# Two linear-attention and gated layers on one core: x-first loads, Strassen products for K in layer two, and earlier heads of the gate/up stages

## The chip, the cores and the metric

The kernel runs on one core of a Trainium2 chip. The number is device time in microseconds (us), from the first to the last instruction of one execution with what lies around it; lower is better. The core has a matrix engine (TensorE, PE in the profile; its weight loads are PEld), VectorE (DVE), ScalarE (ACT), GpSimd (POOL) and SyncE (SP), whose queue issues all DMAs of this kernel. Each engine works through its own list of instructions in order and waits on semaphores.

## What is computed

```python
def _A_ref(x, wqkv, wo):          # S = 2048, D = 1024, 32 heads of 32
    q, k, v = split(x @ wqkv)
    phi = lambda t: jnp.where(t > 0, t + 1, jnp.exp(t)) + 1e-6
    pq, pk = phi(q), phi(k)
    kv = einsum("bhsd,bhse->bhde", pk, v)
    z = einsum("bhsd->bhd", pk)
    o = einsum("bhqd,bhde->bhqe", pq, kv) / (einsum("bhqd,bhd->bhq", pq, z)[..., None] + 1e-6)
    return o @ wo
def _B_ref(x, w_gate, w_up, w_down):   # F = 3584
    return ((x @ w_gate) * (x @ w_up)) @ w_down
x = x + _A_ref(_layernorm(x), A_wqkv, A_wo)
x = x + _B_ref(_layernorm(x), B_w_gate, B_w_up, B_w_down)
x = x + _A_ref(_layernorm(x), A_wqkv, A_wo)
x = x + _B_ref(_layernorm(x), B_w_gate, B_w_up, B_w_down)
```

## The kernel before

The 2048 tokens are 16 tiles of 128. The normalised x is kept transposed in SBUF (`xnT`), x itself in `x_res`, all of it inside one array, `arena`; PSUM (`ps`) has eight banks of 512 columns. The kernel is one long Python program: `P.add(engine, ...)` appends an instruction to an engine's list, with the bytes and banks that it reads and writes, and a planner places the waits. So the order of the calls is the order on each engine, and nothing else decides it. The weights' rows and columns are cut into 2 x 2 blocks, and most large products are made by Winograd's form of Strassen's method: seven block products (1, 5, 6, 2, 7, 3, 4 in the order used) in place of eight, with sums of blocks prepared on DVE.

**Layer A, first time** (`layer_A`, `first`). Tile by tile, K and Q are made with plain products of eight matmuls for each half of 512 columns (`proj`, L949 to L957), phi is taken out of PSUM by `phi_evac` (L649): an exponential of each half on ACT, a minimum on DVE, and one DVE instruction for each half that takes the maximum with 0 and adds. `z_add` (L971) adds K's phi to a running sum on POOL. Layernorm runs ahead, in steps: `start` (two `bn_stats` halves, their aggregate, two short POOL instructions), `b_one` (the normalisation), `step_t` (the transposes on PE and a copy on ACT, later a DMA transpose). `lnstep` (L1220) places these steps around the K products. At the very start SP issues x tile 0 in halves, then k0, x1, k1, x2, q0, x3, q1 and the rest of x (L2182 to L2196); k0, k1, q0, q1 are the column halves of the K and Q weights, 1 MB each, and a tile of x is 256 KB. `pt_ops` (L1246) makes the four sums of Q's weights on DVE during the K products of tiles 4 to 7 and stores them (2 MB, `pt_scratch`) for layer two; the buffer is the one that V's weights are loaded into later (`load_w("v")`, L1280).

**Layer A, second time** (`kq_pairs`, L997 to L1201). Tiles go in pairs. K pairs are plain (`plain`, L1053): four steps of eight matmuls; both halves of a tile are evacuated together, as 128x1024 (`fin2`, L1033). Seven of the Q pairs are Strassen pairs (`strassen`, L1100): seven steps of four matmuls on banks A, B, C, Dk. Step 1's result is copied by ACT from A to B, step 5's to SBUF (`p5`), steps 6 and 7 add into B and DVE joins B and `p5` into Dk and C (`join`, L1118), and each half is evacuated alone (`fin1`, L1045) because `SEP` names Q. `s_sums` (L1080) makes the sums of x blocks for two pairs, four DVE instructions, into the places of `x_res` that are free. The exponentials go through four buffers (`ebuf`, L1019). Every step gets a position, the steps are sorted by it and called (L1172 to L1200); `flow_step` places layernorm's steps and `xr_load` the loads of normalised x for the next stage in the same list. `KSTR` chooses Strassen for K; it is off. What this stage reads is loaded during the end of the layer before (`dticks1`, L2121), behind the down product "3".

**Then** come the products of G (`gchunk`, 16 matmuls each), their use with V's weights (`kvt`), and y, attention's output: for each tile two groups of eight matmuls (`y_grp`, L1379) in the loop at L1399. During that loop layernorm for the gate/up stage runs, and `x_budget` makes the sums of x blocks on DVE from a list (`XQ`).

**Layer B** (`layer_B`): `gateup` runs a hand-written order of tokens (`ORDERS`): P, D and M are products and evacuations of first-level blocks, "11", "16", "17" and the like steps of a product that is itself a Strassen product (second level, 256 columns, L1540), S their sums, T the ticks of other work, R loads of the next weights. A "+" means the next pair. The tokens before the first pair's main work are a head (`pro`), which `pro_step` issues one PE instruction group at a time inside the stage before: one call in the last step of the y loop, three in the last products of the first `down` of layer two. In layer one's first half the head is empty (`jit`). `down` multiplies by w_down, partly with two levels (`two_level`, L1886).

## Time and profile before

| what | value |
|---|---|
| median of 3 runs | 1447.18 us (1445.64 to 1447.4) |
| the profiled execution | 1446.97 us, span 1445.2 us |
| TensorE's granted clock | 1.000 |
| PE busy, DVE busy | 1433.9 us, 1128.6 us |
| ACT busy, POOL busy | 680.2 us, 227.5 us |
| first K product of layer one | 7.93 us |
| K/Q stage of layer two | 737 to 835 us |

The profile is of one execution. A timeline row gives the start in us from the span's start, the duration in us, the engine, the line of the program, the operation, output and input with their shape, and in brackets the idle time before it and what ended it; "x8" merges eight such instructions. A row of the chain of waits has start, duration, engine and line. A row of a group has the busy time in us and the mean of one in ns. A row of a table of stretches has the stretch, its length, the busy time of PE, PEld, DVE, ACT and POOL with their instructions, the granted clock, the mean busy share of the DMA engines and GB/s. A matmul's duration contains its way through the array; the next one starts earlier than it ends, so a hole in PE is read from start to start.

### The profile page before, as it was taken

Reading aid. Unit: us, or ns where it says so; the run is one execution under the profiler, and the core shown is the slowest. Engines: PE = TensorE matmul, PEld = TensorE weight load, DVE = VectorE, ACT = ScalarE, POOL = GpSimd, SP = SyncE. Lnnn points to the kernel's source line nnn. Section 1 sums busy time; section 2 is a strip of 40 time slices with the busy share of each in tenths; the row PEclk is TensorE's granted clock in tenths of the full one; section 3 lists DMA queues with packets and bytes.
Section 4 is the critical chain, followed back from the end, with each engine's and each line's share of the span. In section 5 each row is a group of like instructions: output and inputs, shape, how many; then the busy total and the mean of one; then the engine's idle time right before and its main releaser. Section 6 shows DMA issues by size and latency. Waiting matters only on the chain.

```text
span 1445.2 us, 21993 instructions
## 1 busy us (share of the span) xinstructions
PE 1433.9 (99%) x8294; PEld 800.4 (55%) x8294; DVE 1128.6 (78%) x2027; ACT 680.2 (47%) x1438; POOL 227.5 (16%) x260
## 2 busy tenths in 40 slices
PE   8999999999999999999999999999999999999999
PEld 3444444555544555554664444456666457666547
DVE  6766889889867799877677779879877786777856
ACT  3652256677720255550156423567777005777401
POOL 4543733000000000000044346300000000000000
PEclk9999999999999999999999999999999999999999
DMA  6334757987879899986896067679975779887657
GB/s 233 88 79 118 151 125 155 290 298 249 294 288 338 262 271 294 293 257 225 253 341 195 0 173 151 155 213 274 282 260 197 241 247 296 264 264 257 205 164 239
DMA packets 377993, 324.41 MB, mean 224 GB/s; under 512 B 178208, under 2 KB 326048, under 8 KB 377632
## 3 DMA queue, kind: packets, MB, share of 16 engines
q1 hardware_dynamic: 377888, 323.02, 74.5%
q8 instruction: 65, 1.06, 0.3%
q14 instruction: 40, 0.33, 0.1%
HBM read 237.24 MB, written 62.13 MB: 207 GB/s over the span
## 4 chain that ended last, share of the span: by engine, by line
PE 92%; DVE 4%; DMA 2%; ACT 1%; issue 0%; SPq 0%; POOL 0%; DVEq 0%
PE ps L1470 25%; PE ps L1540 17%; PE ps L2020 16%; PE ps L1291 8%; PE ps L954 6%; PE ps L1383 6%; PE ps L1918 6%; PE ps L945 4%; PE ps L1115 3%; DVE arena L821 2%; DVE arena L824 1%; DMA arena<-in_A_wqkv_dram 1%; DMA arena<-in_B_w_up_dram 1%; DMA arena<-in_B_w_down_dram 1%; PE ps L1303 0%
## 5 line engine op out<-in xcount | busy, mean ns | idle before, releaser
L821 DVE TENSOR_TENSOR arena<-arena 128x512 f16<-128x512 f16 (+7 forms) x752 | 414.1, 577 | 75.9 <-ACT arena L1584 47.6
L1470 PE MATMUL ps<-arena 128*128 128x512 f16 x1808 | 446.5, 379 | 0.7 <-ACT ps L1500 0.7
L824 DVE SCALAR_TENSOR_TENSOR arena<-ps,arena 128x512 f16<-128x512 f32 (+2 forms) x448 | 298.8, 686 | 76.0 <-PE ps L2020 52.2
L1540 PE MATMUL ps<-arena 128*128 128x256 f16 x2324 | 311.8, 273 | 1.7 <-DVE ps L1559 1.3
L1540 PEld LDWEIGHTS ps<-arena 128*128 128x128 f16 (+1 forms) x2324 | 226.2, 98 | 105.0 <-DVE ps L1559 5.8
L1470 PEld LDWEIGHTS ps<-arena 128*128 128x128 f16 (+1 forms) x1808 | 176.4, 98 | 141.8 <-ACT ps L1500 1.4
L2020 PE MATMUL ps<-arena 128*128 128x512 f16 (+1 forms) x1120 | 243.2, 379 | 0.0
L2020 PEld LDWEIGHTS ps<-arena 128*128 128x128 f16 x1120 | 109.6, 98 | 131.3
L1475 ACT ACTIVATE arena<-ps 128x512 f16<-128x512 f32 x224 | 134.0, 598 | 94.0 <-PE ps L1470 90.8
L1556 ACT COPY ps<-ps 128x256 f32<-128x256 f32 x220 | 81.1, 369 | 128.5 <-PE ps L1540 121.4
L1559 DVE TENSOR_TENSOR ps<-ps,arena 128x256 f32<-128x256 f32 x220 | 92.3, 428 | 36.5 <-PE ps L1540 18.4
L474 POOL TENSOR_SCALAR arena<-arena 128x1 f32<-128x1 f32 x48 | 19.5, 407 | 626.1 <-DVE arena L473 626.1
L954 PE MATMUL ps<-arena 128*128 128x512 bf16 x512 | 112.5, 379 | 3.8 <-DMA arena<-in_A_wqkv_dram 1.1
L1291 PE MATMUL ps<-arena 128*128 128x512 bf16 x512 | 115.4, 379 | 0.0
L1383 PE MATMUL ps<-arena 128*128 128x512 bf16 x512 | 111.0, 379 | 0.0
L1922 ACT COPY ps<-ps 128x256 f32<-128x256 f32 x32 | 11.4, 357 | 209.2 <-PE ps L1918 147.1
L1214 POOL TENSOR_TENSOR arena<-arena 128x1024 f16<-128x1024 f32 x32 | 79.2, 2476 | 70.2 <-DVE arena L1212 69.0
L1500 ACT COPY ps<-ps 128x512 f32<-128x512 f32 x112 | 64.2, 573 | 52.0 <-PE ps L1540 44.5
L1918 PE MATMUL ps<-arena 128*128 128x256 f16 (+1 forms) x784 | 87.0, 273 | 0.1
L978 POOL TENSOR_TENSOR arena<-arena 128x512 f32<-128x512 f32 x60 | 74.8, 1266 | 74.1 <-DVE arena L1040 44.0
L954 PEld LDWEIGHTS ps<-arena 128*128 128x128 f16 x512 | 49.5, 98 | 63.0 <-DMA arena<-in_A_wqkv_dram 1.6
L1383 PEld LDWEIGHTS ps<-arena 128*128 128x128 f16 x512 | 50.1, 98 | 60.2
(77 smaller groups left out, 1215.6 us busy)
## 6 DMA issues: line engine op xcount, KB each, us to landing
arena<-w_scratch SPq DMA_DIRECT2D x84, 512.0 KB, 4.9
arena<-sp_scratch SPq DMA_DIRECT2D x56, 512.0 KB, 5.8
arena<-t_scratch SPq DMA_DIRECT2D x29, 896.0 KB, 6.8
arena<-in_B_w_down_dram SPq DMA_DIRECT2D x21, 896.0 KB, 6.9
w_scratch<-arena SPq DMA_DIRECT2D x28, 512.0 KB, 6.5
sp_scratch<-arena SPq DMA_DIRECT2D x28, 512.0 KB, 4.1
arena<-in_B_w_gate_dram SPq DMA_DIRECT2D x42, 256.0 KB, 5.0
arena<-in_B_w_up_dram SPq DMA_DIRECT2D x42, 256.0 KB, 3.2
```

The lines of the kernel that those rows point to most:

```text
L821: P.add("dve", lambda e: e.tensor_tensor(out=out, in0=a, in1=b, op=op), rd=rd, wr=wr, prd=prd)
L824: P.add("dve", lambda e: e.scalar_tensor_tensor(out=out, in0=a, scalar=sc, in1=b, op0=ALU.mult, op1=op1), rd=rd, wr=wr, prd=prd)
L954: return [e.matmul(psb(bank), xnT[:, k, i * 128:(i + 1) * 128], w[:, k, :], start=(k == 0), stop=(k == KT - 1)) for k in range(KT)]
L1291: return [e.matmul(psb(bank), xr[:, t, j * 128:(j + 1) * 128], pk[:, h, t, :], start=(t == 0), stop=(t == NST - 1)) for t in range(NST)]
L1383: return [e.matmul(psb(bank), xnT[:, g, i * 128:(i + 1) * 128], wp[:, g, dh * 512:(dh + 1) * 512], start=(dh == 0 and g == 0), stop=(g == ...
L1470: P.add("pe", lambda e: [e.matmul(psb(bank), w[:, k, :], x[:, k, :], start=(start and k == 0), stop=(k == 3), skip_group_check=True) for k ...
L1475: P.add("act", lambda e: e.activation(t, psb(bank), AF.Copy, scale=SG), prd=[bank], wr=r)
L1540: P.add("pe", lambda e: [e.matmul(psb(bank)[:, 256 * half:256 * half + 256], w[:, k, :], xx[:, k, :], start=(start and k == 0), stop=(k == ...
L1556: P.add("act", lambda e: e.copy(psb(dst[c])[:, 0:256], lo), prd=[bk], pwr=[dst[c]])
L1559: P.add("dve", lambda e: e.tensor_tensor(out=psb(dst[c])[:, 256:512], in0=lo, in1=c5, op=ALU.add), prd=[bk], rd=rc5, pwr=[dst[c]])
L1918: P.add("pe", lambda e: [e.matmul(psb(bank)[:, 256 * half:256 * half + 256], a[:, k, :], w[:, k, :], start=(start and k == 0), stop=(k == ...
L2020: return [e.matmul(psb(bank), hv[:, 7 * hf + k, t * 128:(t + 1) * 128], w[:, k, :], start=(start and hf == 0 and k == 0), stop=(hf == 1 an ...
```

## The change

Six edits, in the order of the program:

1. Settings: `KSTR` on with `KP0 = 4`, so K's pairs 4 to 7 are Strassen pairs and K is evacuated by halves there; three buffers for exponentials, since the fourth's place holds Q's `p5`; the order of the K/Q stage is one written list, `KQ_SEQ`. In it K50 is step 0 of K's pair 5, S60 the first sum for pair 6, L a layernorm step, X a load of x; V, W and O are loads of weights.
2. `fin1` and `fin2` do not issue their instructions any more but put them on a list; after each K or Q step those that were on the list before it are issued. So they stand one step later, behind the join of that step.
3. In layer one `pt_ops` runs for K too, behind that for Q: four sums, one store.
4. The start: x1 is loaded ahead of k0, x2 ahead of k1, x3 ahead of q0, x4 and x5 ahead of q1. Tile 1's first `bn_stats` half goes ahead of tile 0's normalisation. K's first halves of tiles 0 and 1 are issued with the transposes of tiles 1 and 2 between them, then the second halves; from tile 2 on K goes ahead of Q.
5. Heads: layer one's first product "P1A+" goes ahead of y's last group but two; in layer two three steps of the head go ahead of y's last three groups; in `two_level` a fourth step goes ahead of one more group.
6. The loads ahead of layer two: one block of Q's weights (512 KB) moves to the end of the K/Q stage, the four blocks of K's sums (2 MB) are added.

```diff
-    KSTR = False
-    QLAG = 0.284
-    QEND = 0.102
-    SEP = "q"
-    LNP = (0.474, 0.5)
-    SPOS = 0.283
-    SSTEP = 0.14
+    KSTR = True
+    NEB = 3
+    KQ_SEQ = "K00 S00 S01 K01 S02 S03 L K02 K03 K10 L X K11 Q00 K12 Q01 X L Q02 K13 Q03 Q04 K20 X S20 Q05 S21 K21 S22 L Q06 S23 Q10 K22 X Q11 Q12 K23 Q13 L K30 X Q14 S40 Q15 S41 K31 S42 Q16 S43 Q20 X L K32 Q21 Q22 K33 Q23 X K40 Q24 L K41 Q25 K42 Q26 X K43 Q30 K44 K45 L Q31 K46 X Q32 Q33 K50 Q34 S60 K51 Q35 S61 L X S62 K52 S63 Q36 K53 Q40 K54 Q41 X K55 Q42 L K56 Q43 K60 Q44 K61 X Q45 K62 Q46 K63 L Q50 K64 X Q51 K65 Q52 K66 Q53 K70 L X Q54 K71 Q55 K72 Q56 K73 X Q60 K74 L Q61 K75 Q62 K76 Q63 X Q64 L Q65 Q66 V W O"
+    SEP = "qk"
...
-    KP0 = 1
+    KP0 = 4
...
             for h in range(2):
+                if h and mid is not None:
+                    mid()
...
-                OP5 = {"k": RC, "q": RC + 2048 if KSTR else RC + 2 * SZ_SLOT + 4096}
+                OP5 = {"k": RC, "q": RE + 6144 if KSTR else RC + 2 * SZ_SLOT + 4096}
...
+                pend, left = [], {}
+
+                def flush():
+                    while pend:
+                        pend.pop(0)()
+
                 def ebuf():
-                    r = e_cnt[0] % 4
+                    r = e_cnt[0] % NEB
                     e_cnt[0] += 1
+                    if left.get(O_E[r], 0):
+                        flush()
...
+                def fin2(*a):
+                    pend.append(lambda: fin2_(*a))
+
+                def fin1(*a):
+                    pend.append(lambda: fin1_(*a))
...
+                for _, _, tk, f in run:
+                    if tk[0] not in "KQ":
+                        f()
+                        continue
+                    if tk[2] == "0":
+                        flush()
+                    n = len(pend)
                     f()
+                    for _ in range(min(n, len(pend))):
+                        pend.pop(0)()
+                flush()
...
             if first:
                 lnp.start(0)
-                lnp.b_one()
-                lnp.start(1)
+                lnp.start(1, lnp.b_one)
...
+            if first:
+                b0, b1, b2, b3 = next_banks(4)
+                kq_i[0] += 4
+                ev = [phi_evac(b, [k_dst(i, h) for h in range(2)]) for i, b in enumerate(((b0, b1), (b2, b3)))]
+                proj_kh(0, 0, b0, range(4))
+                lnp.step_t(1)
+                proj_kh(0, 0, b0, range(4, KT))
+                ev[0][0](0)
+                lnp.b_one()
+                lnp.start(3)
+                proj_kh(1, 0, b2)
+                ev[1][0](0)
+                lnp.step_t(1)
+                for i, b in enumerate((b1, b3)):
+                    proj_kh(i, 1, b)
+                    ev[i][0](1)
+                    ev[i][1]()
+                    z_add(i)
+                lnp.b_one()
+                lnp.start(4)
...
                 nxt.step_t(1)
+                if not first and i == NST - 1:
+                    pro_step(pro, 1)
                 y_grp(tok[i], 0, i)
...
                 y_seed(i + 1)
+                if i == NST - 2 or not first and i == NST - 1:
+                    pro_step(pro, 1)
                 if i < NST - 1:
                     nxt.b2_one()
-                if i == NST - 1:
-                    pro_step(pro, 1)
...
-                npro = 0 if jit else [tk[:2] in early for _, tk in seq].index(False)
+                npro = [tk[:2] in early for _, tk in seq].index(False)
+                if jit:
+                    npro = 1
+                    seq.insert(0, seq.pop([tk for _, tk in seq].index("P1A+")))
...
-                            if q == "3" and i in (3, 4) and (i == 4 or p):
+                            if q == "3" and i in (3, 4):
                                 pro_step(pro, 1)
...
                     elif t == 1:
                         if KSTR:
-                            load_t("k", 0, 2)
+                            load_q(1, 1)
...
                     else:
                         load_t("q", 1, 2)
                         load_t("q", 3)
-                        if not KSTR:
+                        if KSTR:
+                            load_t("k", 0, 2)
+                            load_t("k", 2, 2)
+                        else:
                             load_q(0, 1)
...
+        xload(1)
         load_w("k", 0)
-        xload(1)
+        xload(2)
         load_w("k", 1)
-        xload(2)
+        xload(3)
         load_w("q", 0)
-        xload(3)
+        xload(4)
+        xload(5)
         load_w("q", 1)
-        for i in range(4, NST):
+        for i in range(6, NST):
             xload(i)
```

More of the change, by code (lines that the diff above doesn't have):

```diff
@@ L1043, in fin2, with fin1_ @@
                         z_add(i)
[L1045 removed]
+                def fin1_(kind, i, h, eb, bank, up, z=False):
+                    left[eb] -= 1
                     d, r = (q_dst if kind == "q" else k_dst)(i, h)
@@ L1257, in layer_A @@
             ptq = (pt_ops("q") + (pt_ops("k") if KSTR else [])) if first else []
-            seq = [("k", i) for i in range(NHOLD)]
+            seq = []
             for i in range(NHOLD, NST):
-                pair = [("k", i), ("q", i - NHOLD)]
-                seq += pair[::-1] if first and i < NPE_T else pair
-            if not first:
+                seq += [("k", i), ("q", i - NHOLD)]
+            if first:
[15 more added lines that the diff above has]
+                    ev[i][1]()
+                    z_add(i)
+                lnp.b_one()
+                lnp.start(4)
+            else:
                 kq_pairs()
```

88 lines of the change are left out of this document (50 added, 38 removed).

## The prediction

> **What bounds the kernel now.** I read the page's busy times, the chain of waits in order of time, then PE's and DVE's timelines at the five places that the change touches, and the table of stretches for the load of the other engines.
>
> ```profile
> span 1445.2 us, 21993 instructions
> PE 1433.9 (99%) x8294; PEld 800.4 (55%) x8294; DVE 1128.6 (78%) x2027; ACT 680.2 (47%) x1438; POOL 227.5 (16%) x260
> ...
> 18.55 6.91 PE ps L954 x32
> ...
> 1410.10 32.24 PE ps L1918 x294
> ```
>
> TensorE sets the time: it is busy 99% of the span. The two rows of the chain that ended last give its step: 6.91 / 32 = 0.216 us from one 512-column matmul to the next, 32.24 / 294 = 0.110 us for one of 256 columns. So only two things can make the kernel faster: fewer matmuls at 0.216 us, or a hole in PE closed. They can make it slower only by opening holes. The terms below are these, in order of time.
>
> **1. Start: x first, K's two halves split.** Before, k0 is issued ahead of x1.
>
> ```profile
> 5.77 0.55 DVE L504 TENSOR_SCALAR arena<-arena 128x1024 f16<-128x1024 bf16 x1 [1.00 <-POOL arena L476]
> 6.37 0.62 PE L588 MATMUL ps<-arena 128*128 128x128 f16 x8 [0.56 <-DVE arena L504]
> 7.93 1.90 PE L954 MATMUL ps<-arena 128*128 128x512 bf16 x8 [0.94 <-ACT arena L590]
> 7.98 1.42 DVE L471 BATCH_NORM_STATS2 arena<-arena 128x6 f32<-128x512 bf16 x2 [1.67 <-DMA arena<-in_A_x_dram]
> ...
> 10.65 0.55 DVE L504 TENSOR_SCALAR arena<-arena 128x1024 f16<-128x1024 bf16 x1 [1.00 <-POOL arena L476]
> 10.98 1.90 PE L954 MATMUL ps<-arena 128*128 128x512 bf16 x8 [1.15 <-DMA arena<-in_A_wqkv_dram]
> 11.71 1.42 DVE L471 BATCH_NORM_STATS2 arena<-arena 128x6 f32<-128x512 bf16 x2 [0.51 <-DMA arena<-in_A_x_dram]
> ...
> 13.41 1.01 ACT L598 COPY arena<-ps 128x1024 f16<-128x1024 f16 x1
> 14.47 3.63 PE L954 MATMUL ps<-arena 128*128 128x512 bf16 x16 [1.15 <-ACT arena L598]
> ```
>
> x1 has landed at 7.98 (DVE starts on it, released by the DMA), k1 at 10.98, x2 at 11.71; x2's quarter megabyte took 0.75 us. PE has two holes, of about 1.2 us each: before 10.98 it waits for k1, before 14.47 for tile 1's copy out of PSUM. At 18.55 (the first row above) it has done K of tiles 0 and 1 and the transposes of tiles 0 to 2.
>
> In the new order x0, x1, k0 are the same 1.5 MB that had landed at 7.98, so k0 is there at about 8.0 and x1 about 4 us sooner; x2 at 8.75; k1 behind it, at x2's old 11.7. Tile 0's chain is held up at most by one half of a bn_stats (0.71 us), which fits between its aggregate and L504 at 5.77. Tile 1's other half runs from 6.3; from the start of the full bn_stats at 7.98 to L504 at 10.65 it took 2.67 us, so from the half about 2.0: L504 at 8.35, transposes at 8.95, copy (0.62 for eight transposes, 1.01 for the copy, 0.1 between) done at 10.7. PE: half of K0h0 from 8.0 to 8.9, transposes to 9.4, the other half to 10.25, hole to 10.7, K1h0 to 12.4, transposes of tile 2 to 12.9, K0h1 and K1h1 (k1 has been there for 1.2 us) to 16.3. The same work is done at 16.3 that was done at 18.55: **-2.2 us**. Bounds: if k1 comes a microsecond later than its slack, -1.2; without the remaining 0.5 us hole, -2.7. q1 moves behind x4 and x5 and lands near 19.8 by x2's rate (2.75 MB after 11.7); Q0's second half now starts about 21.9, since K2 goes ahead of Q0. That cover is 2 us.
>
> **2. Layer one pays for K's sums.** Four subtractions of 128x2048 on DVE and one 2 MB store come behind the ones for Q.
>
> ```profile
> 64.35 1.80 DVE L821 TENSOR_TENSOR arena<-arena 128x2048 f16<-128x2048 bf16 x1
> ...
> 81.47 0.55 DVE L497 TENSOR_SCALAR arena<-arena 128x1024 f16<-128x1024 bf16 x1 [2.46 <-POOL arena L487]
> 102.85 1.26 SPq L433 DMA_DIRECT2D arena<-in_A_wqkv_dram  x2
> 117.29 6.91 PE ps L1291 x32
> ...
> PE ps L954 <- DVE arena L662: 0.5, 1, 0.5
> DMA to landing us min/median/max: 6.8/9.0/10.3
> ```
>
> 4 x 1.80 = 7.2 us of DVE, one in each of four K steps of 6.91 us. There DVE idles up to 2.46 us a step, so they hide; if that cover were gone, 7.2 us. Q's four opened one PE hole of 0.5 us; K's fall where ScalarE's layernorm chain is nearly over. I take **+0.3**, bounds 0 and +1.0. The store reads the buffer that V is loaded into: issued near 100 and landed within 10.3, it delays V's loads (102.85 before) to about 110, plus some 5 us each; the first use of V stands behind two G groups of 16, at 117.29 + 6.91 = 124.2. The first sum for K writes what Q's store reads, but two K steps, 13.8 us, after Q's last sum, and a store lands within 10.3.
>
> **3. Heads of the gate/up stages.** PE waits at each stage's start for an evacuation of the first product.
>
> ```profile
> 242.20 1.03 PE L1470 MATMUL ps<-arena 128*128 128x512 f16 x4
> 243.89 6.22 PE L1470 MATMUL ps<-arena 128*128 128x512 f16 x28 [0.67 <-ACT ps L1500]
> ...
> 960.83 0.38 PE L1540 MATMUL ps<-arena 128*128 128x256 f16 x2
> 961.76 1.92 PE L1540 MATMUL ps<-arena 128*128 128x256 f16 x14 [0.55 <-DVE ps L1559]
> ...
> 1203.26 1.92 PE L1540 MATMUL ps<-arena 128*128 128x256 f16 x14
> 1205.33 1.48 PE L1540 MATMUL ps<-arena 128*128 128x256 f16 x12
> ```
>
> Layer one: four matmuls end at 242.20 + 4 x 0.216 = 243.06, the next runs at 243.89: hole 0.83. The product now goes ahead of y's last group but two, so that ScalarE's copy is long done: **-0.8**. Layer two, first pass: two matmuls end at 961.05, next 961.76: 0.71; with one early product ahead of each of the last three groups of 1.73 us, the DVE join is hidden: **-0.7**. Second pass: 14 matmuls end at 1204.80, next 1205.33: 0.53; one product comes one group (7 x 0.110 = 0.77 us) sooner. I take **-0.35**, bounds 0 and -0.53. Nothing but one ScalarE copy and one step of the queue of x sums moves with these; their banks (0, 4, 5) are not y's banks there.
>
> **4. K/Q stage of layer two.** A plain pair has 32 matmuls of 512 columns, a Strassen pair 28; four pairs: 16 x 0.216 = **-3.45 us**. It pays with two joins, two ScalarE copies and evacuation by halves in each pair.
>
> ```profile
> core 0: us, PE busy (x) PEld busy (x) DVE busy (x) ACT busy (x) POOL busy (x), PEclk, DMA share, GB/s
> ...
> 737.00:786.00 49.00, 48.77 (x226) 21.70 (x224) 37.02 (x54) 33.43 (x61) 27.67 (x36) 1.00 0.91 277
> 786.00:836.00 50.00, 50.00 (x234) 22.50 (x232) 35.16 (x53) 23.19 (x39) 17.46 (x15) 1.00 0.08 29
> ```
> ```profile
> 799.16 0.68 DVE L1050 SCALAR_TENSOR_TENSOR arena<-ps,arena 128x512 bf16<-128x512 f32 x1
> 799.76 0.68 DVE L821 TENSOR_TENSOR arena<-arena 128x1024 f16<-128x1024 f16 x1
> 800.36 0.68 DVE L1050 SCALAR_TENSOR_TENSOR arena<-ps,arena 128x512 bf16<-128x512 f32 x1
> ...
> 801.56 0.43 DVE L647 TENSOR_SCALAR arena<-arena 128x1024 bf16<-128x1024 bf16 x1
> 802.02 1.23 DVE L1040 SCALAR_TENSOR_TENSOR arena<-ps,arena 128x1024 bf16<-128x1024 f32 x1
> 803.16 0.69 DVE L1119 TENSOR_TENSOR ps<-ps,arena 128x512 f32<-128x512 f32 x1
> ...
> 805.88 0.29 DVE L645 TENSOR_SCALAR arena<-arena 128x512 bf16<-128x512 bf16 x1 [2.03 <-ACT arena L1031]
> 806.21 0.69 DVE L1050 SCALAR_TENSOR_TENSOR arena<-ps,arena 128x512 bf16<-128x512 f32 x1
> ...
> 830.92 1.22 DVE L647 TENSOR_SCALAR arena<-arena 128x512 bf16<-128x512 bf16 x1 [0.67 <-ACT arena L1031]
> ```
>
> Start to start, a half phi (L1050), and a sum (L821), occupy DVE 0.60 us, a whole minimum 0.46, a whole phi 1.14, a half minimum 0.33; the join (L1119) is a PSUM operation of L1050's shape and length, 0.60. A plain K pair: 2 x (0.46 + 1.14) = 3.2. A Strassen K pair: 2 x 0.60 + 4 x (0.33 + 0.60) = 4.9. A Strassen Q pair: 2 x 0.60 + 0.33 + 4 x 0.60 = 3.9. From K40 on there are 28 K steps and 31 Q steps of four matmuls, 59 x 0.864 = 51.0 us of PE. DVE: 4 x 4.9 + 31/7 x 3.9 + 4 x 0.60 for the last sums = 39.3 us, 77% of it. In the second half before, DVE had 35.16 of 50.00 and PE did not wait. ScalarE's copies, even at the 1.01 us of L598's of twice the size, add 8 x 1.01 = 8.1 us to 23.19 of 50.00.
>
> So the rate is there, and what counts is the queue: PE's third product (st7) may not write bank B until the join of two K steps before has read it, about 2.6 us later. The deferral of phi's end puts that join ahead of the phi emitted before it, which is at most 0.93 us in DVE's queue. The worst place is K50 to K54, with four sums among the joins: from K46's end to K52's join DVE has two halves with their minimum (0.93 each), two Q joins, two Q phis, three sums and the join itself, 6.7 us, and PE reaches K54 after ten steps, 8.6 us. I take **+0.3** of new holes. Bounds: -0.23 (all the idle time of PE that the first stretch shows goes) and +3.7, below. Three buffers for the exponentials in place of four: K and Q hold two each at the most and are half a pair apart, so the one reused has ended two steps before; its cost is in the same bound.
>
> The 2 MB of K's sums are loaded with layer two's weights, 0.5 MB less goes there for Q:
>
> ```profile
> 748.06 3.27 SPq L582 DMA_TRANSPOSE arena<-arena  x1
> ```
>
> At the stretch's 277 GB/s the 1.5 MB push SP's copies of x and the first of the last eight transposes from 748 to about 753.5. The first four are wanted by the sums S40, which stand after 32.8 us of PE's work, near 770: covered by 16 us, of which three further transposes at most 3.27 each take 10. V's load now follows the last K product by four Q steps and no longer waits for K at the end; it gains cover.
>
> **Sum.** -2.2 + 0.3 - 0.8 - 0.7 - 0.35 - 3.45 + 0.3 = -6.9 us. The profiled execution took 1446.97 us around its span of 1445.2; the median of the three runs is 1447.18, 0.21 above. So 1440.1 by the profile's own time, **1440.3** by the median. The bounds together: -2.7 + 0 - 0.8 - 0.7 - 0.53 - 3.45 - 0.23 = -8.4 and -1.2 + 1.0 - 0.8 - 0.7 - 3.45 + 3.7 = -1.45, so 1438.8 to 1445.7.
>
> **Rivals.**
>
> DVE becomes the bound of K/Q. The row at 830.92 is a half minimum that took 1.22 us instead of 0.29 while GpSimd was adding z (829.72 to 831.99):
>
> ```profile
> 829.72 2.27 POOL L978 TENSOR_TENSOR arena<-arena 128x512 f32<-128x512 f32 x2 [2.83 <-DVE arena L1040]
> ...
> L978 POOL TENSOR_TENSOR arena<-arena 128x512 f32<-128x512 f32 x29 | 34.6, 1212 | 45.0 <-DVE arena L1040 44.0 <-DVE arena L1050 1.0
> ```
>
> GpSimd is busy with those 34.6 us of the stage, 1.21 us each. If each of K's 16 half minima met one, DVE would need 16 x 0.89 = 14.2 us more: 53.5 against 51.0, so 2.5 of holes and one add's length, 1.2, of latency, +3.7 in place of +0.3: 1443.7. For it: z of one token is added while the next token's half phi is evicted, and halves meet it twice as often as wholes. Against: L645's halves before met it rarely (0.29 at 805.88), and there are as many GpSimd adds as before. [...]
>
> The start's gain is lost later in layer one, where the layernorm chain over ScalarE and GpSimd, and not PE, would set the pace up to 62 us: 1440.3 + 2.2 = 1442.5. Against: the chain is issued behind K's exponentials and moves with them.
>
> Slower: the joins queue. From K40 on there are 16 joins, K's and Q's, and behind each a product of both kinds waits. If each came 0.75 us late (behind one more sum or phi than its 2.6 us allow), that is 12 us: 1447.18 - 7.2 + 12 = 1452.0. It decides from a mean lateness of 7.2 / 16 = 0.45 us. Against: joins before, at 70% load, let PE go on without a hole.
>
> That K's Strassen does not do what it says would show as 452 four-step matmuls left; I see no path to it.
>
> **Chances.** Forecast 0.64, DVE-bound 0.13, start lost 0.12, joins 0.07, the rest 0.04, about no change. What a measurement of this kernel can tell from no change is 0.2%, 2.9 us: faster means under 1444.3. The forecast and the lost start lie there almost wholly, of the DVE case two thirds: faster 0.83, within 0.11, slower 0.06. Range: 1437.8 (the lower bound and a microsecond for the scatter of the runs) to 1444.8, which takes in the DVE case.
>
> **What would show it.** K2's first matmul near 16.3 us; layer two's K/Q stage some 3 us shorter, with PE free of waits on L1119; no PE hole over 0.3 us at the three stage starts. Wrong it would be if PE waits for DVE's joins from 786 on, or if layer one's K/Q ends less than 1.5 us sooner.

## The result, and the profile after

The changed kernel took 1442.17 us (median of 6 runs, 1440.57 to 1444.45), the kernel before in the runs beside it 1447.29 (6 runs, 1445.64 to 1449.32): a ratio of 0.9965, 95% interval 0.9952 to 0.9978. That is 5.1 us less, where 6.9 were forecast. A second set of runs of the same changed kernel (e_again, below) gave 1440.83 against 1447.71, which is 6.9 us less: 0.9957, 0.9944 to 0.9969. The profiled execution took 1442.63 us, its span 1440.6: 4.6 us shorter than the span before.

First the page of the changed kernel:

```profile
span 1440.6 us, 22014 instructions
PE 1429.9 (99%) x8278; PEld 799.0 (55%) x8278; DVE 1143.3 (79%) x2053; ACT 685.3 (48%) x1446; POOL 229.9 (16%) x260
```

TensorE is still the bound. DVE has 14.7 us more work than before (1143.3 against 1128.6), PE has 4.0 us less. To see where the time went, I took the first start of PE's work of each stage from both timelines and subtracted. A stage's length is then free of what came before it.

| from, to (first PE starts) | before | after | difference |
|---|---|---|---|
| start of the span, first G of layer one | 117.12 | 114.92 | -2.20 |
| first G, first y of layer one | 69.82 | 69.82 | 0.00 |
| first y, first down of layer one | 221.22 | 221.31 | +0.09 |
| first down, first K product of layer two | 328.83 | 329.57 | +0.74 |
| first K product, first G of layer two | 98.33 | 95.41 | -2.92 |
| first G, first y of layer two | 69.82 | 70.14 | +0.32 |
| first y, first down of layer two | 214.95 | 214.36 | -0.59 |
| first down, end of PE | 322.23 | 322.20 | -0.03 |

The start of the timeline after (PE, DVE and ACT; start, duration, engine, line, operation, in brackets the idle time before and what ended it):

```profile
5.73 0.55 DVE L508 TENSOR_SCALAR arena<-arena 128x1024 f16<-128x1024 bf16 x1 [0.45 <-POOL arena L480]
6.19 0.69 DVE L475 BATCH_NORM_STATS2 arena<-arena 128x6 f32<-128x512 bf16 x1
6.33 0.69 PE L592 MATMUL ps<-arena 128*128 128x128 f16 x8 [0.52 <-DVE arena L508]
...
8.13 0.55 DVE L508 TENSOR_SCALAR arena<-arena 128x1024 f16<-128x1024 bf16 x1 [1.00 <-POOL arena L480]
8.56 1.02 PE L959 MATMUL ps<-arena 128*128 128x512 bf16 x4 [1.53 <-DMA arena<-in_A_wqkv_dram]
...
9.42 0.61 PE L600 MATMUL ps<-arena 128*128 128x128 f16 x8
9.86 1.03 PE L959 MATMUL ps<-arena 128*128 128x512 bf16 x4
10.06 1.01 ACT L602 COPY arena<-ps 128x1024 f16<-128x1024 f16 x1 [2.15 <-PE ps L600]
...
11.13 1.90 PE L959 MATMUL ps<-arena 128*128 128x512 bf16 x8 [0.24 <-ACT arena L602]
...
12.87 0.61 PE L600 MATMUL ps<-arena 128*128 128x128 f16 x8
13.31 5.56 PE L959 MATMUL ps<-arena 128*128 128x512 bf16 x25
```

This is the planned order, row for row: half of K of tile 0, the transposes, the other half, a short hole for the copy (0.24), tile 1, transposes, and then no hole. K's 16 matmuls of second halves start at 13.31, so the next work starts at 13.31 + 16 x 0.216 = 16.77; before, it stood at 18.55. That is -1.8. All of it is about half a microsecond later than forecast, since k0 landed at 8.56.

The rest of the 2.2 us, 0.4, lies at 61 us. The first two rows are the timeline before, the third the one after:

```profile
54.69 6.64 PE L954 MATMUL ps<-arena 128*128 128x512 bf16 x30
61.87 10.30 PE L954 MATMUL ps<-arena 128*128 128x512 bf16 x47 [0.55 <-DVE arena L662]
```
```profile
54.70 17.64 PE L959 MATMUL ps<-arena 128*128 128x512 bf16 x81
```

The hole of 0.55 us that stood behind one of Q's sums is gone, and K's sums opened none. The kernel before with the new start alone (e_start, below), which makes Q's sums too, has no hole between 50 and 66 us either: so the new start closed it.

Layer two's K/Q stage. First the waits of PE on others between 700 and 760 us (line waited for: us in all, times, longest), then rows of PE's timeline, then a table of stretches:

```profile
PE ps L949 <- DMA arena<-in_A_wqkv_dram: 1.6, 2, 1.0
```
```profile
735.62 1.90 PE L949 MATMUL ps<-arena 128*128 128x512 bf16 x8 [0.58 <-DMA arena<-in_A_wqkv_dram]
738.54 8.81 PE L949 MATMUL ps<-arena 128*128 128x512 bf16 x40 [1.02 <-DMA arena<-in_A_wqkv_dram]
...
779.13 52.07 PE L1140 MATMUL ps<-arena 128*128 128x512 bf16 x240
```
```profile
779.13:831.03 51.90, 51.90 (x241) 23.27 (x240) 44.63 (x78) 30.07 (x52) 20.85 (x21) 1.00 0.32 95
```

Two things are to be seen. PE waits twice for K's weights at the stage's start, 1.6 us in all, which it did not do before (8 matmuls of 0.216 us from 735.62 end at 737.35, and the next starts at 738.54: the second hole is 1.2 us from start to start). And from 779.13 it runs 240 matmuls without one hole, through all four Strassen pairs of K: 240 x 0.216 = 51.8 of the 51.90 us. DVE is busy for 44.63 of these (86%).

### The profile page after: what moved, and what is told of

It reads as the page before. It is cut to its first block, busy times and chain, and to the rows that moved or that the text cites. A ratio compares the mean times of both kernels' runs of the same rounds, so it can differ in the third digit from the quotient of the medians.

```text
span 1440.6 us, 22014 instructions
## 1 busy us (share of the span) xinstructions
PE 1429.9 (99%) x8278; PEld 799.0 (55%) x8278; DVE 1143.3 (79%) x2053; ACT 685.3 (48%) x1446; POOL 229.9 (16%) x260
## 3 DMA queue, kind: packets, MB, share of 16 engines
q8 instruction: 65, 1.06, 0.3%
## 4 chain that ended last, share of the span: by engine, by line
PE 91%; DVE 5%; DMA 2%; SPq 0%; ACT 0%; issue 0%; POOL 0%; DVEq 0%; ACTq 0%
PE ps L1530 26%; PE ps L1600 17%; PE ps L2083 16%; PE ps L1441 8%; PE ps L959 8%; PE ps L1981 5%; PE ps L1349 5%; PE ps L1140 5%; PE ps L949 2%; DMA arena<-in_A_wqkv_dram 1%; DVE arena L1245 1%; DVE arena L825 1%; DVE arena L1248 1%; DVE arena L828 1%; DMA arena<-in_B_w_up_dram 1%; DMA arena<-in_B_w_down_dram 1%
## 5 line engine op out<-in xcount | busy, mean ns | idle before, releaser
L825 DVE TENSOR_TENSOR arena<-arena 128x512 f16<-128x512 f16 (+8 forms) x756 | 419.2, 581 | 76.2 <-ACT arena L1644 47.6
L983 POOL TENSOR_TENSOR arena<-arena 128x512 f32<-128x512 f32 x60 | 78.6, 1330 | 67.5 <-DVE arena L1073 29.6
```

The source lines that it names most:

```text
L825: P.add("dve", lambda e: e.tensor_tensor(out=out, in0=a, in1=b, op=op), rd=rd, wr=wr, prd=prd)
```

## The experiments

Every experiment is the changed kernel with one edit, or the kernel before with one part of the change. They answer five questions.

**The start alone.** e_start is the kernel before with the change's edit 4 and nothing else.

```diff
-        load_w("k", 0)
-        xload(1)
+        xload(1)
+        load_w("k", 0)
...
-                lnp.start(0)
-                lnp.b_one()
-                lnp.start(1)
+                lnp.start(0)
+                lnp.start(1, lnp.b_one)
...
```

> The kernel before with the start of the change alone: x first, K's halves split, K ahead of Q. Theory: layer one's G starts 2.2 us sooner than in the kernel before (117.1 to 114.9), 1.6 of it from the start itself and 0.6 because the hole near 61 us closes; K's weights of layer two come in time, since Q's blocks are behind them as in the kernel before, so layer two's K/Q starts 2.1 us sooner without a hole: 1445.1. Rival (the full DMA engines set the start of layer two): G 2.2 us sooner, but the start of layer two's K/Q with 1.6 us of holes, 1446.7.

It took 1446.52 against 1447.18: ratio 0.9993, 0.9984 to 1.0003. Of the two microseconds only 0.7 were left, and the interval takes in no change at all. The profile shows why in its first rows and in the stretches of 2 us (PE, PEld, DVE, ACT, POOL busy, granted clock, DMA share, GB/s):

```profile
6.87 0.62 PE L590 MATMUL ps<-arena 128*128 128x128 f16 x8 [1.58 <-DVE arena L506]
8.71 1.86 PE L957 MATMUL ps<-arena 128*128 128x512 bf16 x4 [1.22 <-DMA arena<-in_A_wqkv_dram]
10.37 1.06 PE L598 MATMUL ps<-arena 128*128 128x128 f16 x8
11.22 1.14 PE L957 MATMUL ps<-arena 128*128 128x512 bf16 x4
```
```profile
8.00:10.00 2.00, 1.29 (x4) 0.48 (x5) 1.23 (x2) 0.38 (x1) 0.57 (x1) 0.51 1.09 351
10.00:12.00 2.00, 2.00 (x14) 1.29 (x12) 0.94 (x4) 0.53 (x1) 0.79 (x2) 0.64 1.09 359
```

Four K matmuls took 1.86 us, where they took 1.02 in the changed kernel's profile, and the granted clock was 0.51 and 0.64. G of layer one started at 116.32, not 114.92. The same fall, to 0.50, stands in the profiles of e_kplain, e_loads and e_loads2, with G at 115.99, 116.66 and 117.92.

**What makes PE slow at the start.** PE idles ahead of 8.5 us in two pieces, 0.52 and 1.53 us after, 1.58 and 1.22 in e_start. e_warm fills the second with seven matmuls whose result nobody reads; e_warm2 also makes the ten warming matmuls at the very start thirteen; e_start_warm is e_start with the seven; e_cold is the changed kernel with two of the ten left, and without the seven. e_again is the changed kernel as it is, run beside e_warm.

```diff
                 lnp.step_t(1)
+                P.add("pe", lambda e: [e.matmul(psb(B_KVT[1]), wrm[:, 0:128], wrm, start=True, stop=True) for _ in range(7)],
+                      rd=R(O_A[0], 1024), pwr=[B_KVT[1]])
```
```diff
-    PE_WARM = 10
+    PE_WARM = 13       # e_warm2 (2 in e_cold)
```

> The changed kernel with seven matmuls of zeros more, behind the transposes of tile 0, so that PE works from 6.8 to 8.3 us in place of standing until K's first weights land. In three of the five profiles with the new start the granted clock fell to 0.50 for about 3 us from 8 to 13 us; in the profile of the changed kernel itself and in that of the kernel before it did not. Theory: PE's idle time ahead of K's first product makes TensorE's clock fall in about half of the runs, for 1.2 to 2 us each; with the matmuls the clock is 1.00 in every run, G starts at 114.9 us or sooner, and the median is 1441.3, 1 us below the changed kernel's beside it. Rival: the clock's fall has nothing to do with that idle time (some runs of the kernel before have it too); then half of the runs still show less than 1.000, and the median is the changed kernel's within 0.4 us.

> The changed kernel once more, beside the two runs above, for its time on the same chip and a second look at what varies: the clock at the start (1.00 or a stretch at 0.50), the holes at the start of layer two's K/Q (1.9 us or less than 0.5) and the length of layer one's gate/up stage. Expected: 1442.3, and a K/Q stage of 94.2 to 95.5 us from the first K product to G.

> The kernel before with only the new order of the start, and seven dummy matmuls of 512 columns between tile 0's transposes and the first product of K. Theory: the start is worth about 1.6 us where the granted clock stays at 1.00, and the runs without the dummies lost most of it to a clock of 0.50; then the first G starts near 115.0 to 115.5 (116.3 without the dummies, 117.1 before), no stretch of the first 16 us shows a clock under 1.00, and the median is 1.5 to 2.5 us under the kernel before. Rival: the start's gain is lost later in layer one whatever the clock does; then the median is within 0.8 us of the kernel before.

> The changed kernel with 13 warming matmuls in place of 10 at the very start and seven more before the first product of K. Theory: with PE's idle time before 8.5 us filled from both sides the clock stays at 1.00 in nearly every run; median 1440.0 to 1441.0, ratio near 0.995, and no run at a reduced clock. Rival: the clock falls for another reason than PE's idle time at the start; then about half of the runs still show a reduced clock, median 1441.5 to 1442.5.

> The changed kernel with 2 warming matmuls at the very start in place of 10, so that PE idles some 3 us more ahead of 8 us. Theory: PE's idle time ahead of K's first product is what lowers the granted clock; then nearly every run shows a reduced clock (3 of 6, then 3 of 5, did in the changed kernel, 2 of 11 with the gaps filled), the first K products take 1.86 us for four in place of 1.02, the first G starts at 116 to 118 in place of 114.9, and the median is 1442.5 to 1444.5. Rival: the clock falls by chance, whatever PE does; then no more than half of the runs are reduced and the median is 1441 to 1442.5.

| run | median us | beside before's | ratio, 95% interval | runs whose mean clock was under 1.000 |
|---|---|---|---|---|
| changed kernel | 1442.17 | 1447.29 | 0.9965, 0.9952 to 0.9978 | 3 of 6 |
| e_again | 1440.83 | 1447.71 | 0.9957, 0.9944 to 0.9969 | 2 of 5 |
| e_warm | 1440.97 | 1447.71 | 0.9956, 0.9944 to 0.9969 | 1 of 5 |
| e_warm2 | 1440.65 | 1446.65 | 0.9967, 0.9955 to 0.9978 | 2 of 6 |
| e_start | 1446.52 | 1447.18 | 0.9993, 0.9984 to 1.0003 | 4 of 10 |
| e_start_warm | 1445.53 | 1446.65 | 0.9993, 0.9984 to 1.0002 | 0 of 11 |
| e_cold | 1442.22 | 1447.00 | 0.9965, 0.9953 to 0.9978 | 0 of 6 |

With the gap filled the first G came at 114.55 (e_warm), 114.72 (e_warm2) and 114.62 (e_start_warm). Over all kernels with the new start and ten warmers, e_loads aside, the mean clock of a run was under 1.000 in 23 of 52 runs; with the gap filled in 3 of 27, and in the kernel before, beside these experiments, in 14 of 61. That speaks for the idle time as a cause. Within one of these kernels with ten warmers a run under 1.000 took between 0.2 us (e_nohead1, means of 2 and 4) and 3.2 us (e_loads2, 2 and 3) longer; in the changed kernel it was 1.3 (3 and 3).

e_cold seems to contradict this: I expected nearly every run to be under 1.000, and none was. But PE was slow all the same:

```profile
6.36 1.03 PE L592 MATMUL ps<-arena 128*128 128x128 f16 x8 [3.96 <-DVE arena L508]
8.39 1.87 PE L959 MATMUL ps<-arena 128*128 128x512 bf16 x4 [1.00 <-DMA arena<-in_A_wqkv_dram]
10.05 1.06 PE L600 MATMUL ps<-arena 128*128 128x128 f16 x8
10.90 3.41 PE L959 MATMUL ps<-arena 128*128 128x512 bf16 x12
14.15 0.61 PE L600 MATMUL ps<-arena 128*128 128x128 f16 x8
```
```profile
8.00:10.00 2.00, 1.61 (x4) 0.58 (x5) 1.51 (x3) 0.07 (x1) 0.11 (x1) 1.00 1.09 359
10.00:12.00 2.00, 2.00 (x12) 1.29 (x11) 0.97 (x3) 0.85 (x1) 0.79 (x2) 1.00 1.08 358
```

Four K matmuls in 1.87 us and eight transposes in 1.06 (0.61 later), with a granted clock of 1.00 in both stretches. The twelve matmuls from 10.90 to the next transposes at 14.15 took 3.25 us in place of 12 x 0.216 = 2.59, three more of them at half rate at most: so PE ran at half rate until about 12 us, for some 3.8 us from 8.39 on, and the column didn't show it; G started at 116.20, as expected. The column doesn't show it in other profiles either: the changed kernel's ten warming matmuls from 1.37 on took 4.45 us, where 10 x 0.216 is 2.16, and the stretch from 2 to 4 us stands at 1.00. Why it doesn't was not shown. So e_cold's six runs at 1.000 say nothing for or against the theory.

What goes ahead of a fall is shown in part by the rows and stretches of eight profiles with ten warming matmuls and the new start:

| profile | the ten warming matmuls, us | PE busy from 6 to 8 us | granted clock, 8 to 10, 10 to 12, 12 to 14 us |
|---|---|---|---|
| e_start | 3.92 | 0.62 | 0.51, 0.64, 1.00 |
| e_loads2 | 4.01 | 0.62 | 0.55, 0.50, 0.50 |
| e_kplain | 4.38 | 0.62 | 0.74, 0.50, 0.91 |
| changed kernel | 4.45 | 0.69 | 1.00, 1.00, 1.00 |
| e_again | 4.45 | 0.66 | 1.00, 1.00, 1.00 |
| e_nodefer | 4.45 | 0.67 | 1.00, 1.00, 1.00 |
| e_warm | 4.02 | 1.79 | 1.00, 1.00, 1.00 |
| e_start_warm | 4.45 | 1.71 | 1.00, 1.00, 1.00 |

The closest pair is e_loads2 and e_warm, whose warming matmuls took 4.01 and 4.02: with the gap PE was busy for 0.62 us from 6 to 8 and fell to half rate, with the seven matmuls for 1.79 us and did not. So in e_start, e_loads2 and e_kplain two things stood ahead of the fall: the gap, and warming matmuls that took less than 4.45 us, so that some of them ran faster than the others. With the gap and 4.45 us the three other profiles had no fall. How long the warming matmuls take varies from execution to execution, and so does the start of K's first product (7.96 in e_again, 9.06 in e_loads2); that fits with only some runs being hit. No run set how long the warming matmuls take, or tried a gap of another length, so what decides between them is open. So is what happened in the 3 of 27 runs, as none of them was profiled.

The medians don't separate the warmed kernels from e_again: 1440.97 and 1440.65 against 1440.83. What is shown is that PE's slow first products cost 1 to 3 us at the first G, and that they come less often when PE has no gap there.

The start alone, with the clock at 1.00 in all its 11 runs, is worth 1.1 us by the medians (interval -2.3 to +0.3) and 2.5 at the first G of its one profile. Which of these the start is worth isn't settled.

**The heads.** e_nohead1 takes layer one's early product back to its old place; e_warm2_nohead does so in e_warm2.

```diff
                 if jit:
-                    npro = 1
-                    seq.insert(0, seq.pop([tk for _, tk in seq].index("P1A+")))
+                    npro = 0
```

> The changed kernel without the early product of layer one's gate/up stage. In the changed kernel the hole of 0.8 us at the stage's start is gone, but the stage ends no sooner against its start. Theory: what sets the pace there is the landing of the weights of the next pair, whose sums DVE waits for with a join behind them; PE only arrives earlier at that wait. Then without the head the hole at the start is back (0.8 us) and two later ones shrink by as much: the second half of the stage starts within 0.2 us of the changed kernel's 492.4, and the time is the same, 1442.2. Rival: the head is worth 0.8 us and something else in the change was lost there; then 1443.0 and 493.2.

> The kernel of the run before this one, without the early product of layer one's gate/up stage. Theory: that product's gain is given back within the stage (weights that land at 258 and 276 set the pace there), so the two medians lie within 0.4 us of each other, and from y's first product to the next stage 220.4 to 221.8 us pass in both. Rival (the prediction's term): this kernel is 0.8 us slower.

e_nohead1 took 1442.96 (ratio 0.9968, 0.9956 to 0.9979); e_warm2_nohead 1441.65 against e_warm2's 1440.65, with intervals that overlap almost wholly (0.9955 to 0.9980 and 0.9955 to 0.9978). By the medians the kernels without the product are 0.8 us (against the changed kernel) and 1.0 us slower, as the prediction's term says; by the means of the same runs 0.2 and 0.1. So the runs don't decide it; the stage's length does. From the first y to the first down the eight profiles with the early product (e_loads aside) show 221.57 us on average (221.12 to 222.24), the five without it 221.34 (220.43 to 222.33). A gain of 0.8 would have to be seen there. The hole at the start is gone, yet nothing came of it. Where it went stands in the chain of waits (start, us, what; pauses of issue left out), first before, then after:

```profile
252.42 8.03 DMA arena<-in_B_w_up_dram
...
265.10 0.35 DVE ps L1559
...
270.92 7.62 DMA arena<-in_B_w_down_dram
...
282.85 0.35 DVE ps L1559
...
283.25 0.83 PE ps L1540 x6
```
```profile
249.97 8.23 DMA arena<-in_B_w_up_dram
...
262.83 0.35 DVE ps L1619
...
268.64 7.80 DMA arena<-in_B_w_down_dram
...
280.74 0.35 DVE ps L1619
...
281.14 0.83 PE ps L1600 x6
```

Counted from the first y (186.94 before, 184.74 after), w_up's load starts at 65.48 and 65.23, w_down's at 83.98 and 83.90, and PE goes on behind the join at 96.31 and 96.40. PE had been 0.8 us ahead, but the loads weren't: a chain of two loads of 8 us, with sums on DVE between them, sets this point. The 14 profiles bear this out: in 13 of them, four without the early product and nine with it, PE goes on 4.7 us after w_down's load has landed, which is 91.4 to 92.6 us after the first y. In the one left, e_nohead1, the load landed at 90.6 and PE did not wait; this profile has the shortest stage of all, without the early product.

Layer two's heads have their test in the profile of e_start, which has the old ones: from the first y to the first down it takes 214.96 us, after 214.36; from the first down to the end of PE 322.22, after 322.20. So the heads of layer two are worth 0.6 in the first pass (0.15 to 0.65 over the eleven profiles that have them) and nothing in the second. The rows after show what PE does there, first pass and second:

```profile
957.29 1.47 PE L1600 MATMUL ps<-arena 128*128 128x256 f16 x12
959.21 1.48 PE L1600 MATMUL ps<-arena 128*128 128x256 f16 x12 [0.44 <-ACT arena L1644]
```
```profile
1198.91 1.47 PE L1600 MATMUL ps<-arena 128*128 128x256 f16 x12
1200.75 1.48 PE L1600 MATMUL ps<-arena 128*128 128x256 f16 x12 [0.37 <-ACT arena L1644]
```

Twelve matmuls of 0.110 us end at 958.61 and 1200.23: holes of 0.60 and 0.52. Before, the first pass had one of 0.71 and the second one of 0.53. The hole moved one step along and now waits for ScalarE's copy (L1644), not for the join.

**Loads ahead of layer two.** e_loads was to put the loads of q's blocks back behind down's product 3. Its edit was wrong: with the branch for tick 1 gone, that tick fell into the general one and issued the loads of Q's and K's sums a step too early and again later.

```diff
                     if t == 0:
...
-                        if KSTR:
-                            load_q(0, 0)
-                            load_q(1, 0)
-                    elif t == 1:
-                        if KSTR:
-                            load_q(1, 1)
                     elif t == 2:
+                        if KSTR:
+                            load_q(0, 0)
+                            load_q(1, 0)
+                            load_q(1, 1)
```

> The changed kernel with three of Q's weight blocks (q00, q10, q11, 512 KB each) issued again behind the last row of product 3 and not right behind k0 and k1. In the changed kernel PE stands 0.7 us before K's first product of layer two and 1.2 us before the second, each time until a K weight block has landed. Theory: q00 and q10 stand in the same DMA queues right behind k1 and slow it; without them the two holes together fall from 1.9 to 0.5 us or less, the kernel takes 1.4 us less (1440.8). Rival: the DMA engines are full for 30 us ahead of that point, and PE, being 2 us earlier, has run into what they can deliver; then the holes stay at 1.6 to 1.9 us and the time at 1442.2.

1458.12, ratio 1.0077 (1.0059 to 1.0095). PE waited 14.7 us in the down product, by the profile for one of these loads:

```profile
PE ps L1981 <- DMA arena<-pt_scratch: 14.7, 1, 14.7
```

This says nothing of the order it was meant to test. e_loads2 does the same with `elif t == 1: pass` kept:

> The changed kernel with q00, q10 and q11 behind product 3's third step, as in the kernel before, and nothing else moved. Theory: these blocks, queued right behind k1, make k1 late; without them the holes ahead of layer two's first two K products are 0.5 us or less together and the median is 0.7 us below the changed kernel's beside it. Rival, which the last runs speak for (1.9 us of holes in one profile with the new order of loads, less than 0.4 in two others with the same order, 1.2 us more than before in the one with the old order): the holes come and go with the DMA engines' load from run to run, whatever this order; then the medians agree within 0.4 us.

1440.76 (0.9952, 0.9938 to 0.9966), as e_again beside it. PE waited 1.1 us for the weights at the stage's start, e_start with the old order of loads 1.1 us too, the changed kernel 1.6; eight other profiles with the new order show no such wait. So it isn't tied to the order or to K's sums. It comes in some executions and is no price of the change that I could show.

**Strassen for K, and the deferral.** e_kplain has K plain in layer two, with the rest of the change, the written order among it.

```diff
-    KP0 = 4
+    KP0 = 8
...
-    KQ_SEQ = "... K40 Q24 L K41 Q25 K42 Q26 X K43 Q30 K44 K45 L Q31 K46 X ..."
+    KQ_SEQ = "... K40 Q24 L Q25 K41 Q26 X Q30 K42 L Q31 K43 X ..."
```

> The changed kernel with K's pairs 4 to 7 plain again (32 matmuls of 512 columns a pair in place of 28), at the places of every second Strassen step; everything else stays, the loads of K's sums too. Theory: Strassen for K is worth its 16 matmuls and costs nothing, so layer two's K/Q stage is 3.5 us longer (95.4 to 98.9 from the first K product to G) and the kernel takes 1445.6. Rival: the joins and halves cost a part of it that no hole shows, so the stage is longer by 2.5 us or less, 1444.5.

1444.82 (0.9983, 0.9974 to 0.9993). From the first K product to the first G it took 97.83 us, PE without a wait; e_again takes 94.50, also without one, and the six other profiles with Strassen for K and no such wait (e_nodefer, below, aside) 93.99 to 94.63. Strassen for K is worth 3.3 us there (3.2 to 3.8 over these profiles); counted, it is 16 x 0.216 = 3.45.

e_nodefer issues phi's end at once:

```diff
-                    n = len(pend)
                     f()
-                    for _ in range(min(n, len(pend))):
-                        pend.pop(0)()
+                    flush()
```

> The changed kernel with phi's end issued in the step that it belongs to, and not put off by a step. The prediction's reading: the deferral puts the joins ahead of a phi of at most 0.93 us; without it a join comes up to 0.93 us later, and with 16 joins and a slack of 2.6 us a step PE gets holes of 0 to 2 us in all between 745 and 832, most of them with L1125 as the releaser: 0 to 2 us slower than the changed kernel, K to G 94.5 to 96.5. Rival: the joins decide; then every second join holds PE by 0.5 us or more, 4 us and over, K to G 98 or more. Second rival: VectorE's queue has so much slack that nothing changes (K to G 94.5, median within 0.5 of the changed kernel).

1442.75 (0.9975, 0.9965 to 0.9984). The expectation calls the join's line L1125; in the profiles of the changed kernel it is L1144. PE's waits in the stage, and DVE's and PE's rows at the first of them:

```profile
PE ps L1140 <- DVE ps L1144: 1.5, 2, 1.1
```
```profile
796.03 0.69 DVE L1073 SCALAR_TENSOR_TENSOR arena<-ps,arena 128x512 bf16<-128x512 f32 x1
796.63 1.28 DVE L825 TENSOR_TENSOR arena<-arena 128x1024 f16<-128x1024 f16 x2
797.83 0.69 DVE L1144 TENSOR_TENSOR ps<-ps,arena 128x512 f32<-128x512 f32 x1
798.58 0.82 PE L1140 MATMUL ps<-arena 128*128 128x512 f16 x3 [0.47 <-DVE ps L1144]
```

A half phi and two sums stand ahead of the join, and PE waits for it. Two such holes, 0.47 and 1.07 us of idle time, make 1.5 us, from start to start 0.63 and 1.23, and the stage 96.19 us long, 1.7 more than e_again's. The first is ahead of the 24th of the 60 steps that follow each other there from Q23 on, and in the written order that is K54: the very step that the prediction named as the worst. The second is ahead of the last, Q66. The other joins don't hold PE even so.

## Why the prediction held, and where its terms were off

The result lies inside the range and on the forecast's side, 1.9 us above the forecast in the first set of runs and 0.5 above in the second. The largest term was right, the smaller ones were not all, and errors of both signs partly cancel.

- **K/Q, -3.45 + 0.3.** Right. Strassen for K gives 3.3 us, and no new hole opened from 745 to 831, where up to 3.7 had been allowed. The stage in e_again is 3.8 us shorter than before: beyond those 3.3, the holes of the kernel before are gone too, and e_kplain (97.83 against 98.33) puts these at 0.5, not 0.23. The reading of the queue was right as well: with the deferral no join is late, without it 1.5 to 1.9 us are lost.
- **DVE as the bound** did not come. The rival rested on a half minimum of 1.22 us. These are groups of DVE's instructions after, from 779.13 to 831.03 (busy us, mean ns):

```profile
L651 DVE TENSOR_SCALAR arena<-arena 128x512 bf16<-128x512 bf16 x16 | 4.9, 308 | 2.8 <-ACT arena L1046 2.7
L825 DVE TENSOR_TENSOR arena<-arena 128x1024 f16<-128x1024 f16 x4 | 3.4, 871 | 0.0
L649 DVE TENSOR_SCALAR arena<-arena 128x512 bf16<-128x512 bf16 x5 | 2.6, 514 | 0.0
```

  K's 16 half minima took 308 ns on average, so they cost 16 x 0.02 = 0.3 us more than at 0.29, not 14.2. What the rival started from, a half minimum drawn out while GpSimd adds, is there, only not its frequency. Of the 21 half minima in this stretch, the four that began while GpSimd was adding z took 0.54 to 0.92 us, the other 17 took 0.28 to 0.29. Three of the four are Q's; only one of K's 16 is among them, since each of GpSimd's adds waits for the phi of its half and is mostly over before K's next minimum (one took 1.15 us from 812.18, and that minimum began at 813.50). DVE's load was still underestimated: 44.63 us of 51.90, 86% and not 77%. Q's half minima (0.51 on average) and the sums (0.87) were longer than the rows that I took them from for the same reason: one of the four sums, which took 1.46 us, began during an add, and the other three took 0.7. The end of a plain pair falls into the stretch, too. It held all the same.
- **The joins as a queue** did not come either: the mean lateness was nothing with the deferral, and 1.5 / 16 = 0.1 us without, far under the 0.45 from which it would have decided.
- **Start, -2.2.** The mechanism was right and the size 0.4 too large: -1.8 at K2's first matmul (16.77, where 16.3 was forecast), because k0 landed at 8.56 and not at 8.0. That scatters: in e_again the first K product started at 7.96, and K2's first matmul then came at 12.72 + 16 x 0.216 = 16.18, as forecast; in e_loads2 the first K product started at 9.06. What the prediction lacked is PE's rate. It counted 0.216 us for every matmul from 8 us on; in part of the executions the first ones take twice that (four in 1.86 us in e_start, in 1.02 in the changed kernel), and 1 to 3 us are lost at the first G.
- **Start's gain lost later** did not come: the hole at 61 us closed, and the 2.2 us stand unchanged at the first y.
- **K's sums in layer one, +0.3.** Nothing was paid; with the 0.4 gained at 61 us the sum of the first two terms was forecast as -1.9 and came as -2.2.
- **Heads, -0.8, -0.7, -0.35.** They gave 0, -0.6 and 0. The step that failed is "so that ScalarE's copy is long done: -0.8". The copy is done, but the work behind the hole waits further on for loaded weights, and these are no earlier. The prediction gave this term no bounds: -0.8 stands in its best sum and in its worst. In layer two the holes of 0.60 and 0.52 still stand where the prediction's test allowed none over 0.3; in the second pass the hole only moved.
- **Loads of layer two, covered.** The bytes behind the first transposes were covered, as worked out. K's first weights, whose cover I didn't check, were not in three of twelve profiles, among them the one of the changed kernel, where the start of the stage lost 0.74 and the hole behind its first eight matmuls another 1.2. One of the three has the old loads, so I book it as scatter.
- **Not foreseen:** from G to y in layer two 0.3 us more. Ahead of the last of Q's products there, PE's four matmuls of a G group (898.26) took 1.35 us and not 1.03; e_again (70.15), e_loads (70.17) and e_loads2 (70.09) have it too, the others don't (69.8 to 69.9). In e_again the last of these four matmuls waits 0.16 us for DVE's L1396, which empties a bank; why DVE comes later in these profiles wasn't tried.

The sum in the profile: -2.2 (start and K's sums) - 0.6 (one head) - 2.9 (K/Q) + 0.74 + 0.32 + 0.06 = -4.6. Without the two waits for weights it would have been about -6.5, close to the forecast, and e_again's profile, whose first weights came in time in both layers, is 6.9 us shorter than the one before. That nearness is in part luck: 1.25 us of heads never came, and in their place 0.3 for K's sums and 0.3 for new holes in K/Q were not paid, and holes closed that had no term in the forecast, 0.4 at 61 us and 0.5 in K/Q.

## What to carry to other kernels

On this TensorE-bound kernel, 16 matmuls taken away were worth 3.3 us, nearly their count times their step (3.45). That held because DVE's rows showed slack where the new waits fall (busy for 86% of the stretch), and because the join was put ahead of work that nobody waits for (put behind it, PE waited 1.5 us). A hole closed at a stage's head was worth only as much as stayed ahead at the next point that a load sets (0.8 us ahead at the head, nothing behind w_down's load), so follow the chain to the next landing before you count it. Differences of a microsecond need stage lengths from several profiles: one profile has waits of one to two microseconds that the next doesn't have (1.6 us for K's first weights in layer two in the changed kernel's, none in e_again's).

## What the runs showed of the hardware that was not expected

The granted clock in the stretches of a profile did not always show TensorE's rate. In e_cold four matmuls of 512 columns took 1.87 us at a granted clock of 1.00, in e_start 1.86 at 0.51, in the changed kernel 1.02 at 1.00. The mean duration of a row told the rate in all three, the column in two.

A fall to half rate came after two idle stretches of 1.58 and 1.22 us (e_start), in a kernel where PE had worked from 1.37 to about 5.3 us just before. In the three profiles with such a fall that the table above has, the ten warming matmuls took 3.92 to 4.38 us and PE was busy for 0.62 us from 6 to 8; with 4.45 and 0.66 to 0.69, or with 4.02 and 1.79, none came.

A half minimum on DVE that begins while GpSimd adds took 0.54 to 0.92 us in the stretch from 779 to 831 us, any other 0.28 to 0.29.
